# Three tiles of the first expert worked on ahead of the last routing, and the overflow loop inside a condition

## The chip, the core and the metric

One core of a Trainium2 chip runs the whole program in one launch. TensorE (PE) multiplies, its weight loads are listed as PEld; VectorE (DVE), ScalarE (ACT) and GpSimd (POOL) do the rest; SyncE (SP) and the queues of ACT and POOL issue DMAs. The metric is the device time of the launch in microseconds, the median of the runs. A measurement of this kernel tells two versions apart from about 0.2%, which is 2.1 us.

## The reference

Block-causal attention (4 batches, 8 heads, 576 positions, head size 64, blocks of 64) gives 2304 rows of 512. A mixture of experts sends each row to two of eight experts, and a gated MLP follows:

```python
attn = softmax(where(block_i >= block_j, scale * q @ k.T, -1e9)) @ v
x = attn as 2304 rows of 512
noisy = x @ w_gate + log1p(exp(x @ w_noise)) * noise
top2, top2_w = the two largest of 8, softmax over them
for e in range(8): out[mask] += top2_w * (maximum(x[mask] @ w1[e], 0) @ w2[e])   # 512 -> 1024 -> 512
h = out @ w_in                                                                   # 512 -> 2048
out = (h * clip(h + 3, 0, 6) / 6) @ w_out                                        # 2048 -> 512
```

## The kernel before

Everything is float32 on the outside. Each operand is split into a high and a low part (fp32r), and a product is three matmuls: high by high, low by high, high by low. A split is a copy on ACT (`split_hi`, `x_hi`, `h_hi`) and a subtraction on DVE (`split_lo`, `x_lo`, `h_lo`).

**Attention.** It runs over pairs of heads, batch by batch. Its order is not that of the code: each step is given to a `Plan` (a list scheduler in Python, run when the program is built) with its engine, an estimated cost, the steps that it needs and a priority (table `PR`); the plan writes the steps in the order that it finds, and that is the order of each engine's queue. When a batch is through, its gate logits are summed up (`lsum`, L858, in the tile `lgp`; matmuls `lgm`, L863 to L865) and its rows are routed (`route`). The attention's output rows are stored to the table `x_tok` in DRAM, from which rows are gathered by token number with indirect DMAs on POOL.

**The ahead stage.** The routing of the last batch is a long chain of small DVE steps. So that PE has work meanwhile, the first `AHEAD` tiles of expert 0 (128 rows each) are taken from the first three batches alone: `early_load` (L424) gathers them into `raw_q` and `raw_k`, buffers that the attention no longer needs, PE transposes them (`x_tr`, L401), and a second plan (`plan2`) interleaves expert 0's two matrix products over them with the last routing. A product has eight parts f of 128 hidden columns: `s1` (L433 to L435) is 12 matmuls per f, with the width of the tiles as their columns; `s2` (L1136 to L1138) three matmuls of 512 columns per f and tile. The remaining tiles of expert 0 (`load_x`, L1105, into `xn`) need the routing of all four batches; their gathers and transposes are at the end of `plan2`. Splits of the experts' weights into high and low (wa for the first matrix, wb for the second, by pairs of f) are steps of both plans; `PRE` says which of them the first plan makes.

**The experts.** 72 steps g (`NG`) follow, written out in code order: g = 0 to 7 is expert 0 over its remaining columns (624 are kept for it in all, `CAPS`), then experts 1 to 7, the last in two halves. The weights of the next expert are loaded in pairs from expert 0 on. A generator (`route_rows`, `rr` in the loop) makes, two pieces per step, the lists with which rows are turned later on, and the list of rows that are over an expert's capacity; `overflow_count` then loads their number into a register of every engine. **Overflow.** Just ahead of the last product of expert 7 (g = 72), `overflow()` runs a loop over those rows (L1254). For these inputs the number is zero, and the body never runs; the loop's branches and its waits do.

Last comes the MLP in five groups of rows.

Of the kernel before, what the change touches and what calls it, by code (L numbers as in the profile page):

```python
# [31 lines left out]
HB = 4  # L32
# [4 lines left out]
FIRST_TURNED = 2  # L37
TURN_X = (((), ()), ((), (0, 1)), ((), (2,)), ((0,), ()), ((1,), (3,)), ((2,), (4,)), ((3, 4), ()), ((), ()))
CONV = (8, 5)
STICK = 2.77  # L40
TURN = {(a, b): t for b, r in {"S": {"T": 0.045, "V": 0.083, "F": 0.086, None: 0.084}, "V": {"T": 0.134, "S": 0.072, "F": 0.086, None: 0.09},
                               "T": {"V": 0.038}}.items() for a, t in r.items()}
SELS = ({"DVE": 0.17}, {"POOL": 0.6}, {"DVE": 0.17, "POOL": 0.6}, {"POOL": 0.6, "DVE": 0.17})
PRE = ((0, 0), (1, 0))
WLS = ({"DVE": 1.2}, {"DVE": 1.14, "POOL": 2.4}, {"POOL": 2.4, "DVE": 1.14}, {"POOL": 2.4})
VHS = ({"POOL": 2.3}, {"DVE": 0.42}, {"POOL": 2.3, "DVE": 0.42}, {"DVE": 0.42, "POOL": 2.3}, {"ACT": 0.65, "DVE": 0.42})
PR = {'v': -317.22, 'qk': -13.33, 'keep': 1, 'S': -2.19, 'max': -82.24, 'exp': -40.31, 'pt': 0.29, 'hi': 360.75, 'lo': -37.22, 'hid': True, 'av': 7.35, 'o': 252.33, 'od': True, 'inv': 36.95, 'fin': 28.78, 'x': -1.53, 'route': -0.9, 'rp': 1, 'route2': 6.36, 'xt': 83.29, 'eg': 587.2, 'ex': 432.13, 'ew': 2149.25, 'first': 0, 'sel': 2, 'vh': 3, 'wl': 0, 'wa': -64.03, 'wb': 20.81, 'h': -79.68, 's2': -28.75, 'vs': (-0.62, -2.53, 0.92, 0.17, 0.59, -5.66), 'vpt': (28.74, 8.73, -37.77, -2.51, -5.17, 6.9, -0.23, 1.96), 'vp': (-2.81, -6.08), 'vf': (15.46, 3.5)}
CLAMP = 122879.9921875


# [7 lines left out]
class Plan:  # L58
# [97 lines left out]
def kernel(  # L156
# [15 lines left out]
    B, H, S, D = v.shape  # L172
# [5 lines left out]
    NF = F // 128  # L178
# [28 lines left out]
    k_in, k = k, {}  # L207
# [44 lines left out]
    NP2 = H // 2  # L252
# [46 lines left out]
    ohsum = [const.tile([128, E], BF16, name=f"ohsum{i}") for i in range(B)]  # L299
# [78 lines left out]
    w_s = {}  # L378
# [255 lines left out]
    with actx:  # L634
# [359 lines left out]
                                  lambda g: tb[g.bank],  # L994
                                  NU * NP2 * (b + 1) + PR["route2" if b == B - 2 else "route"])[0]
        for t in range(AHEAD):
            key = ("qk"[t], 0)
            k["eg", t] = add({"POOL": 1.04}, lambda e, t=t, key=key: early_load(t, raw[key]),
                             [k["r", B - 2], k["X", NPAIR - NP2 - 1]] + ([k["kl", NPAIR - 2]] if t else [k["ql", NPAIR - 2, h] for h in range(2)]), PR["eg"] + t, lat=2.4)
            g = Bank("t", PR["keep"])  # L1000
            tr = add({"PE": 0.44}, lambda e, t=t, g=g: x_tr("a", xn["a", t], t, AHEAD * 128, tb[g.bank].rearrange("p (k n) -> p k n", k=KD)), [k["eg", t]], PR["ex"] + t, take=g)
            hi_ = add({"ACT": 0.48}, lambda e, t=t, g=g: x_hi("a", t, tb[g.bank].rearrange("p (k n) -> p k n", k=KD)), [tr], PR["ex"] + t, drop=g)
            k["ex", t] = add({"DVE": 0.6}, lambda e, t=t, g=g: x_lo("a", t, tb[g.bank].rearrange("p (k n) -> p k n", k=KD)), [hi_], PR["ex"] + t, drop=g)
# [247 lines left out]

    def overflow():
        lst, nov, total = ovf["lst"], ovf["nov"], ovf["n"]
        with tc.For_i(0, total, 1) as j, tc.tile_pool(name="ov", bufs=1) as op_:  # L1254
            cur = op_.tile([128, 2], F32, name="cur")
            for r in range(2):
                nc.vector.tensor_copy(cur[:, r:r + 1], lst[:, r, bass.ds(j, 1)])
# [85 lines left out]
    k2 = {}  # L1343
# [22 lines left out]
    for f in range(NF + 1):  # L1366
        pr = 10 + 2 * f
        if f < NF and f % 2 == 0:
            k2["wa", f // 2] = wops(0, f // 2, [k2.get(("s1", f - 4 + i)) for i in range(2)], pr + PR["wa"])
        if f < NF and f % 2 == 0:  # L1370
            k2["wb", f // 2] = wops(1, f // 2, [k2.get(("s2", f - 4 + i)) for i in range(2)], pr + PR["wb"])
        if PR['first'] <= f < NF:
            g = Bank("h", 1)

            def first(e, f=f, g=g):
                g.tile = s1("a", f, f // 2, 0, n_)

            def second(e, f=f, g=g):
                hT["a", f] = h_tiles()
                h_hi(hT["a", f], g.tile, 0, n_)  # L1380

            k2["s1", f] = add({"PE": 1.31}, first, [k2.get(("wa", f // 2))], pr, take=g)
            hh = add({"ACT": 0.27}, second, [k2["s1", f], k2.get(("s2", f - HB))], pr + PR["h"], drop=g)
            k2["h", f] = add({"DVE": 0.34}, lambda e, f=f, g=g: h_lo(hT["a", f], g.tile, 0, n_), [hh], pr + PR["h"], drop=g)
        if f:
            k2["s2", f - 1] = add({"PE": 1.3}, lambda e, f=f - 1: s2(range(AHEAD), hT.pop(("a", f)), w_s[1, f // 2], f,
                                                                     f == 0, f == NF - 1),
                                  [k2.get(("h", f - 1)), k2.get(("wb", (f - 1) // 2)), k2.get(("s2", f - 2))], pr + PR["s2"])
    counts = work.tile([128, 16], F32, tag="counts", name="counts", bufs=1)[:, 0:E]
# [39 lines left out]
    wops(0, NPF, [k2["s1", NF - 4], k2["s1", NF - 3]], 50)
    wops(1, NPF, [k2["s2", NF - 4], k2["s2", NF - 3]], 51)  # L1430
# [11 lines left out]
    for g in range(NG + 1):  # L1442
        u = NPF + g // 2 + 1
        if g < NG:
            e, f, _, _ = STEPS[g]
            if g % 2 == 0:
                split(0, u)
            if f == 0 and e + 1 < E:
                for t in range(NT):
                    load_x(e + 1, t)  # L1450
            if wide and g == CONV[0] - 1:
                conv_load(0)
            if g % 2 == 1:
# [12 lines left out]
        if wide and g >= CONV[0]:
            for _ in range(CONV[1]):
                next(conv, None)
        if g == NG:
            overflow()  # L1470
        if g:
            e_s2(g - 1)
        if g == NG - NF:
            for t in range(len(GR[0])):
                gather(0, t)
        for _ in range(2):
            if next(rr, None) == 0:
                overflow_count()
        if g < NG and f >= 2 and f - 2 < NT and e + 1 < min(E, FIRST_TURNED):
            x_tile(e + 1, xn.pop((e + 1, f - 2)), f - 2, CAP)  # L1480
        if g < NG and FIRST_TURNED <= e + 1 < E:
            outs, ins = TURN_X[f]
            for t in outs:
                e_out(e + 1, t)
            for t in ins:
                e_in(e + 1, t)
        if NG - NF + 4 <= g < NG - NF + 4 + len(GR[0]):
            combine(0, g - (NG - NF + 4))
        if NG - NF + 5 <= g < NG - NF + 5 + len(GR[0]):
            combined(0, g - (NG - NF + 5))  # L1490
# [93 lines left out]
```

## Time and profile before

| | us |
|---|---|
| median of 3 runs (1068.59 to 1070.15) | 1069.24 |
| the profiled execution: own time | 1069.84 |
| its span, first to last instruction | 1068.0 |
| PE busy | 1051.7 |
| DVE busy | 778.2 |
| ACT busy | 593.3 |
| POOL busy | 316.5 |

The mean granted clock of TensorE in the span is 0.993. The profiled execution's own time is 1.84 us more than its span, and 0.60 us over the median. Times below are microseconds from the span's start. A row of the timeline gives start and duration; matmuls are pipelined, so a matmul of 256 columns is listed with 0.28 us and starts 0.12 us behind the one ahead of it. "[0.85 <-DMA xn...]" means that the engine sat idle 0.85 us before this instruction, and what released it.

### The profile page before, as it was taken

What the parts mean: (1) busy time and instruction counts of PE and PEld (TensorE: products, weight loads), DVE (VectorE), ACT (ScalarE), POOL (GpSimd) and SP (SyncE); (2) the same over time, 40 slices, a digit from 0 to 9 for tenths busy, and PEclk for the clock granted to TensorE, in tenths of its full rate; (3) what the DMA queues carried; (4) which work ended last, traced back from release to release, by engine and by line L of the source; (5) the groups of instructions that cost most, each with busy time, mean ns of one, the idle gap of its engine ahead of it and who ended that gap; (6) DMA issues with size and microseconds to landing.
All of it is one profiled execution on the core that took longest, in us unless ns stands there. A gap on an engine that the chain in (4) does not pass through costs nothing. (4 is left out here: it accounts for less than half of the span.)

```text
span 1068.0 us, 16961 instructions
## 1 busy us (share of the span) xinstructions
PE 1051.7 (98%) x6069; PEld 923.8 (86%) x6069; DVE 778.2 (73%) x1471; ACT 593.3 (56%) x1121; POOL 316.5 (30%) x378
## 2 busy tenths in 40 slices
PE   8999999999999999999999999999999999999998
PEld 6999999987988999999888898988888888888886
DVE  8878787887598898988787855875745755665442
ACT  6777777764456555655555444654535444454442
POOL 7558787723101120202020001743401421310000
PEclk8999999999999999999999999999999999999999
DMA  7534432114999999987787525212202211201001
GB/s 185 148 96 129 130 90 53 24 47 150 328 275 331 301 301 280 278 225 255 195 247 202 165 82 176 79 60 60 56 5 69 50 40 48 62 10 40 1 1 40
DMA packets 163573, 141.80 MB, mean 133 GB/s; under 512 B 92373, under 2 KB 131381, under 8 KB 163485
## 3 DMA queue, kind: packets, MB, share of 16 engines
q1 hardware_dynamic: 147501, 102.79, 34.7%
q0 software_dynamic: 8640, 28.32, 8.5%
q10 hardware_dynamic: 7344, 9.57, 2.7%
q8 instruction: 49, 0.80, 0.3%
q14 instruction: 39, 0.32, 0.1%
HBM read 92.94 MB, written 36.70 MB: 121 GB/s over the span
## 5 line engine op out<-in xcount | busy, mean ns | idle before, releaser
L433 PE MATMUL h<-xh,wah 128*128 128x512 f32 (+8 forms) x832 | 272.7, 328 | 0.7 <-ACT xh L404 0.7
L434 PE MATMUL h<-xl,wah 128*128 128x512 f32 (+8 forms) x832 | 271.5, 326 | 0.4 <-issue 0.3
L435 PE MATMUL h<-xh,wal 128*128 128x512 f32 (+8 forms) x832 | 271.5, 326 | 0.0
L1136 PE MATMUL y<-wbh,hh 128*128 128x512 f32 (+1 forms) x576 | 226.3, 393 | 2.1 <-issue 2.1
L1137 PE MATMUL y<-wbl,hh 128*128 128x512 f32 (+1 forms) x576 | 226.0, 392 | 0.0
L1138 PE MATMUL y<-wbh,hl 128*128 128x512 f32 (+1 forms) x576 | 225.5, 392 | 0.0
L433 PEld LDWEIGHTS h<-xh,wah 128*128 128x128 f32 x832 | 156.6, 188 | 16.2 <-ACT xh L404 1.0
L434 PEld LDWEIGHTS h<-xl,wah 128*128 128x128 f32 x832 | 156.7, 188 | 15.5 <-issue 0.5
L435 PEld LDWEIGHTS h<-xh,wal 128*128 128x128 f32 x832 | 156.6, 188 | 11.5
L1138 PEld LDWEIGHTS y<-wbh,hl 128*128 128x128 f32 (+1 forms) x576 | 107.6, 187 | 25.4 <-DVE hl L460 0.8
L1136 PEld LDWEIGHTS y<-wbh,hh 128*128 128x128 f32 (+1 forms) x576 | 107.5, 187 | 23.3 <-issue 2.5
L456 ACT ACTIVATE hh<-h 128x288 fp32r<-128x288 f32 (+7 forms) x128 | 53.0, 416 | 132.1 <-PE h L435 130.9
L1137 PEld LDWEIGHTS y<-wbl,hh 128*128 128x128 f32 (+1 forms) x576 | 107.6, 187 | 20.6
L1498 DVE SCALAR_TENSOR_TENSOR r<-r,h 128x512 f32<-128x512 f32 (+1 forms) x80 | 50.5, 631 | 97.9 <-ACT r L1497 97.7
L1497 ACT ACTIVATE r<-h,three 128x512 f32<-128x512 f32 (+1 forms) x80 | 51.6, 645 | 120.2 <-PE h L435 120.1
L388 DVE TENSOR_TENSOR wal<-wa,wah 128x1024 fp32r<-128x1024 f32 x80 | 106.3, 1328 | 12.1 <-ACT wah L384 10.9
L388 DVE TENSOR_TENSOR wbl<-wb,wbh 128x1024 fp32r<-128x1024 f32 x76 | 102.5, 1349 | 14.6 <-ACT wbh L384 12.8
L384 ACT CAST wbh<-wb 128x1024 fp32r<-128x1024 f32 x80 | 83.8, 1048 | 23.4 <-PE y L1138 13.3
L1501 DVE TENSOR_TENSOR hl<-r,hh 128x512 fp32r<-128x512 f32 (+1 forms) x80 | 57.3, 717 | 51.5 <-ACT hh L1500 51.0
L1500 ACT CAST hh<-r 128x512 fp32r<-128x512 f32 (+1 forms) x80 | 46.2, 577 | 84.7 <-DVE r L1498 83.2
L772 ACT ACTIVATE P<-sb,nm 128x192 f32<-128x192 f32 (+4 forms) x144 | 74.6, 528 | 28.8 <-DVE nm L766 28.8
L384 ACT CAST wah<-wa 128x1024 fp32r<-128x1024 f32 x80 | 83.7, 1046 | 3.0 <-DMA wb<-in_moe_w_dram 2.4
(269 smaller groups left out, 1783.3 us busy)
## 6 DMA issues: line engine op xcount, KB each, us to landing
wa<-in_moe_w_dram SPq DMA_DIRECT2D x23, 512.0 KB
wb<-in_moe_w_dram SPq DMA_DIRECT2D x23, 512.0 KB
y_tab<-yo SPq DMA_DIRECT2D x32, 256.0 KB
w<-in_moe_w_in_dram SPq DMA_DIRECT2D x16, 512.0 KB
y_tab<-zero SPq DMA_DIRECT2D x8, 1024.0 KB
w<-in_moe_w_out_dram SPq DMA_DIRECT2D x16, 512.0 KB
x_tok<-x SPq DMA_DIRECT2D x32, 144.0 KB
wa<-in_moe_w_dram ACTq DMA_DIRECT2D x9, 512.0 KB
```

The lines of the kernel that those rows point to most:

```text
L384: nc.scalar.copy(w_s[which, u][0], raws[PS[u]][which])
L388: (nc.gpsimd if e == "POOL" else nc.vector).tensor_tensor(lo, raws[PS[u]][which], hi.bitcast(F32), op=OP.subtract)
L433: nc.tensor.matmul(ps, lhsT=wh, rhs=xh, start=first, stop=False)
L434: nc.tensor.matmul(ps, lhsT=wh, rhs=xl, start=False, stop=False)
L435: nc.tensor.matmul(ps, lhsT=wl, rhs=xh, start=False, stop=last)
L456: nc.scalar.activation(h[0][:, c0:c1], ps[:, :c1 - c0], AF.Relu)
L772: nc.scalar.activation(o, views.pop((p, i)), AF.Exp, bias=nms.pop((p, i)), scale=1.0, accum_out=rs[p % 3][:, i:i + 1])
L1136: nc.tensor.matmul(yps[t][:n], lhsT=hh[:, sl], rhs=wh[:, f % 2], start=first, stop=False)
L1137: nc.tensor.matmul(yps[t][:n], lhsT=hh[:, sl], rhs=wl[:, f % 2], start=False, stop=False)
L1138: nc.tensor.matmul(yps[t][:n], lhsT=hl[:, sl], rhs=wh[:, f % 2], start=False, stop=last)
L1497: nc.scalar.activation(r[:, :n], ps[:, :n], AF.Relu, bias=three, scale=1.0)
L1501: nc.vector.tensor_tensor(hl[:, :n], r[:, :n], hh[:, :n].bitcast(F32), op=OP.subtract)
```

## The change

- `AHEAD` is 3: a third tile is gathered, into the buffer `raw_v`, once the high and low parts of the pair before the last are made from it, and is part of the ahead stage. `s1` there has 384 columns and `s2` nine matmuls per f; expert 0 after the routing has 240 columns in place of 368, and two late gathers in place of three.
- `PRE` loses (1, 0): the low and high part of the first pair of the second matrix is made in `plan2` and not in the attention.
- Priorities in `PR`: the last batch's routing -75 (before -1000), the ranks 0 (before -900), the last `s1` -30, the late transposes -9 (before 83.29). Costs that the plan assumes for `s1`, `s2` and the splits grow with the width; the assumed latency of the late gathers is 3.6 (before 2.4).
- `RR` = 8: `route_rows` starts at step g = 8.
- The overflow loop is inside `tc.If(total > 0)`.

```diff
-AHEAD = 2
+AHEAD = 3
...
+RR = 8
...
-PRE = ((0, 0), (1, 0))
+PRE = ((0, 0),)
...
     def early_load(t, a):
+        if len(a.shape) > 2:
+            a = a.rearrange("p c h d -> p (c h d)")
...
         for t in range(AHEAD):
-            key = ("qk"[t], 0)
+            key = ("qkv"[t], 0)
+            free = ([k["ql", NPAIR - 2, h] for h in range(2)], [k["kl", NPAIR - 2]], [k["hi", NPAIR - 2], k["lo", NPAIR - 2]])[t]
             k["eg", t] = add({"POOL": 1.04}, lambda e, t=t, key=key: early_load(t, raw[key]),
-                             [k["r", B - 2], k["X", NPAIR - NP2 - 1]] + ([k["kl", NPAIR - 2]] if t else [k["ql", NPAIR - 2, h] for h in range(2)]), PR["eg"] + t, lat=2.4)
+                             [k["r", B - 2], k["X", NPAIR - NP2 - 1]] + free, PR["eg"] + t, lat=2.4)
...
-        with tc.For_i(0, total, 1) as j, tc.tile_pool(name="ov", bufs=1) as op_:
+        with tc.If(total > 0), tc.For_i(0, total, 1) as j, tc.tile_pool(name="ov", bufs=1) as op_:
...
-            k2["s1", f] = add({"PE": 1.31}, first, [k2.get(("wa", f // 2))], pr, take=g)
+            k2["s1", f] = add({"PE": 12 * (n_ / 2400.0 + 0.0145)}, first, [k2.get(("wa", f // 2))], pr if f < NF - 1 else PR["s1"], take=g)
...
-            k2["s2", f - 1] = add({"PE": 1.3}, lambda e, f=f - 1: s2(range(AHEAD), hT.pop(("a", f)), w_s[1, f // 2], f,
+            k2["s2", f - 1] = add({"PE": 0.69 * AHEAD}, lambda e, f=f - 1: s2(range(AHEAD), hT.pop(("a", f)), w_s[1, f // 2], f,
...
-    _, dp = route(B - 1, [], add, lambda: Bank("x", 1), psum, -1000, plan.done[k["lg", B - 1]])
+    _, dp = route(B - 1, [], add, lambda: Bank("x", 1), psum, PR["last"], plan.done[k["lg", B - 1]])
...
-        k2["g", t] = add({"POOL": 1.04}, lambda e, t=t: load_x(0, t), [dp["id"]], -10 + t, lat=2.4)
+        k2["g", t] = add({"POOL": 1.04}, lambda e, t=t: load_x(0, t), [dp["id"]], -10 + t, lat=3.6)
...
-        for _ in range(2):
+        for _ in range(2 if g >= RR else 0):
             if next(rr, None) == 0:
                 overflow_count()
```

The order of GpSimd's queue at the end of the attention: the last sums `lgp` of the gate logits, the early gathers (`raw_q`, `raw_k`, `raw_v`) and the first late gathers. Before:

```order
L585 TENSOR_SCALAR sel_3153<-laneb,pmf 128x128
L424 DMA raw_q_74<-x_tok,ids_152 128x512
L424 DMA raw_k_76<-x_tok,ids_152 128x512
L858 TENSOR_TENSOR lgp_205<-lgp_205,x 64x144 x2
L1017 MEMSET capv 128x1 x8
L1105 DMA xn<-x_tok,ids 128x512 x3
```

And of the change:

```order
L588 TENSOR_SCALAR sel_3153<-laneb,pmf 128x128
L861 TENSOR_TENSOR lgp_205<-lgp_205,x 64x144 x2
L427 DMA raw_q_74<-x_tok,ids_152 128x512
L427 DMA raw_k_76<-x_tok,ids_152 128x512
L427 DMA raw_v_72<-x_tok,ids_152 128x512
L1021 MEMSET capv 128x1 x8
L1109 DMA xn<-x_tok,ids 128x512 x2
```

The two sums stand ahead of the gathers now, a third gather behind them, and two late gathers are left.

TensorE's queue at the same place, where the attention's last transposes (L840, L843 now) end and the ahead stage begins. Before:

```order
L840 MATMUL tb_172<-iw,oT_3257 128x96 x5
L401 MATMUL tb_168<-ident,raw_q_74 128x128 x4
L401 MATMUL tb_171<-ident,raw_k_76 128x128 x4
L863 MATMUL tb_169<-lgp_205,half 128x16
L864 MATMUL tb_169<-lgp_205,half 128x64
L865 MATMUL tb_169<-lgp_205,half 128x64
L433 MATMUL h<-xh_3292,wah_3139 128x256
```

And of the change:

```order
L843 MATMUL tb_172<-iw,oT_3254 128x96 x5
L402 MATMUL tb_168<-ident,raw_q_74 128x128 x4
L402 MATMUL tb_171<-ident,raw_k_76 128x128 x4
L866 MATMUL tb_169<-lgp_205,half 128x16
L867 MATMUL tb_169<-lgp_205,half 128x64
L868 MATMUL tb_169<-lgp_205,half 128x64
L402 MATMUL tb_170<-ident,raw_v_72 128x128 x4
L436 MATMUL h<-xh_3289,wah_3139 128x384
```

The transpose of the third tile stands between the logits and the first product, whose matmuls all read the three tiles together.

TensorE's queue behind the overflow loop, where the last product of expert 7 begins. Before:

```order
L1254 REGISTER_ALU
L1254 COMPARE_AND_BRANCH
L1254 UNCONDITIONAL_BRANCH [waits DMASW5_49,DMASW4_49,DMASW6_49,DMASW3_49,DMASW7_49,DMASW2_49,DMAHW0_49,DMASW1_49,DMAHW1_49,DMASW0_49,DMAHW2_49,SP_sequencer_49,DMAHW3_49,DVE_sequencer_49,DMAHW4_49,PE_sequencer_49,DMAHW5_49,Activation_s
L1136 MATMUL y_7935<-wbh,hh 128x512
```

And of the change:

```order
L1258 UNCONDITIONAL_BRANCH [waits PE_49]
L1140 MATMUL y_7933<-wbh,hh 128x512 [waits Activation_49]
L1141 MATMUL y_7933<-wbl,hh 128x512
L1142 MATMUL y_7933<-wbh,hl 128x512 [waits DVE_49]
```

With the loop skipped, the branch that waits for every engine and DMA queue lies on the path of before; on that of the change lies one that waits for PE's own semaphore, and the first matmuls have waits of their own.

## Rows read from the trace of the kernel before

**Rows 1.** The page: busy time and its share of the span by engine.

```profile
PE 1051.7 (98%) x6069; PEld 923.8 (86%) x6069; DVE 778.2 (73%) x1471; ACT 593.3 (56%) x1121; POOL 316.5 (30%) x378
```

**Rows 2.** Busy time by stretch: PE, PEld, DVE, ACT, POOL, granted clock, DMA share, GB/s.

```profile
220.00:230.00 10.00, 9.26 (x77) 8.72 (x75) 6.81 (x18) 4.72 (x10) 4.34 (x12) 1.00 0.34 86
250.00:260.00 10.00, 8.04 (x47) 6.45 (x47) 7.09 (x12) 3.96 (x7) 8.08 (x7) 1.00 0.65 187
658.00:660.00 2.00, 0.02 (x1) 0.00 (x0) 0.44 (x2) 0.00 (x0) 0.00 (x0) 1.00 0.06 12
```

**Rows 3.** Timeline of POOL, end of the attention.

```profile
220.54 1.22 POOL L424 DMA_INDIRECT raw_q<-x_tok,ids  x1 [5.61 <-DVE ri L827]
222.07 0.94 POOL L424 DMA_INDIRECT raw_k<-x_tok,ids  x1 [0.31 <-issue]
223.04 1.39 POOL L858 TENSOR_TENSOR lgp<-lgp,x 64x144 f32<-64x144 f32 x1
225.99 0.49 POOL L858 TENSOR_TENSOR lgp<-lgp,x 64x144 f32<-64x144 f32 x1 [1.56 <-DMA raw_k<-x_tok,ids]
```

**Rows 4.** Timeline of DVE, beside these.

```profile
222.33 0.55 DVE L847 TENSOR_TENSOR x<-tb,ri 128x384 f32<-128x384 f32 x1
222.92 1.17 DVE L388 TENSOR_TENSOR wbl<-wb,wbh 128x1024 fp32r<-128x1024 f32 x1
```

**Rows 5.** Timeline of PE, start of the ahead stage.

```profile
227.56 0.60 PE L401 MATMUL tb<-ident,raw_q 128*128 128x128 f32 x4
228.00 0.60 PE L401 MATMUL tb<-ident,raw_k 128*128 128x128 f32 x4
229.15 0.40 PE L863 MATMUL tb<-lgp,half 128*128 128x16 f32 x2 [0.55 <-DVE lgp L858]
230.47 0.39 PE L434 MATMUL h<-xl,wah 128*128 128x256 f32 x1
```

**Rows 6.** Timeline of POOL: the first late gather.

```profile
248.63 1.15 POOL L1105 DMA_INDIRECT xn<-x_tok,ids  x1 [21.80 <-PE y L1138]
```

**Rows 7.** Timeline of PE, end of the ahead stage.

```profile
248.44 0.28 PE L433 MATMUL h<-xh,wah 128*128 128x256 f32 x1
...
251.12 0.28 PE L435 MATMUL h<-xh,wal 128*128 128x256 f32 x1
252.25 0.66 PE L401 MATMUL xps<-ident,xn 128*128 128x128 f32 x4 [0.85 <-DMA xn<-x_tok,ids]
...
254.38 0.66 PE L401 MATMUL xps<-ident,xn 128*128 128x128 f32 x4
...
256.26 0.60 PE L401 MATMUL xps<-ident,xn 128*128 128x128 f32 x4
257.59 0.43 PE L433 MATMUL h<-xh,wah 128*128 128x368 f32 x1 [0.73 <-ACT xh L404]
258.31 0.43 PE L434 MATMUL h<-xl,wah 128*128 128x368 f32 x1 [0.29 <-issue]
```

**Rows 8.** Timeline of PE at the overflow loop.

```profile
657.63 0.39 PE L1138 MATMUL y<-wbh,hl 128*112 128x512 f32 x1
660.10 0.68 PE L1136 MATMUL y<-wbh,hh 128*128 128x512 f32 x1 [2.08 <-issue]
```

**Rows 9.** PE's sequencer at line L1254: ns min/median/max, first and last start.

```profile
L1254 PEldq EVENT_SEMAPHORE  x13: 51/51/51, 658.1 to 659.7; - x13
L1254 PEldq COMPARE_BRANCH  x3: 101/187/319, 655.4 to 659.9; - x3
```

**Rows 10.** Busy time by stretch (columns as in rows 2): below full clock.

```profile
660.00:662.00 2.00, 1.90 (x5) 1.48 (x6) 0.00 (x0) 0.33 (x1) 0.00 (x0) 0.56 0.01 4
662.00:664.00 2.00, 2.00 (x11) 1.79 (x10) 1.05 (x2) 1.20 (x2) 0.00 (x0) 0.58 0.34 131
8.00:12.00 4.00, 2.44 (x13) 1.42 (x12) 3.39 (x9) 3.29 (x12) 1.86 (x2) 0.97 0.84 222
12.00:22.00 10.00, 8.40 (x33) 7.43 (x33) 9.10 (x17) 5.47 (x16) 8.18 (x9) 0.50 0.52 123
```

More of the change, by code (lines that the diff above doesn't have):

```diff
@@ L43 @@
 SELS = ({"DVE": 0.17}, {"POOL": 0.6}, {"DVE": 0.17, "POOL": 0.6}, {"POOL": 0.6, "DVE": 0.17})
-PRE = ((0, 0), (1, 0))
+PRE = ((0, 0),)
 WLS = ({"DVE": 1.2}, {"DVE": 1.14, "POOL": 2.4}, {"POOL": 2.4, "DVE": 1.14}, {"POOL": 2.4})
 VHS = ({"POOL": 2.3}, {"DVE": 0.42}, {"POOL": 2.3, "DVE": 0.42}, {"DVE": 0.42, "POOL": 2.3}, {"ACT": 0.65, "DVE": 0.42})
-PR = {'v': -317.22, 'qk': -13.33, 'keep': 1, 'S': -2.19, 'max': -82.24, 'exp': -40.31, 'pt': 0.29, 'hi': 360.75, 'lo': -37.22, 'hid': True, 'av': 7.35, 'o': 252.33, 'od': True, 'inv': 36.95, 'fin': 28.78, 'x': -1.53, 'route': -0.9, 'rp': 1, 'route2': 6.36, 'xt': 83.29, 'eg': 587.2, 'ex': 432.13, 'ew': 2149.25, 'first': 0, 'sel': 2, 'vh': 3, 'wl': 0, 'wa': -64.03, 'wb': 20.81, 'h': -79.68, 's2': -28.75, 'vs': (-0.62, -2.53, 0.92, 0.17, 0.59, -5.66), 'vpt': (28.74, 8.73, -37.77, -2.51, -5.17, 6.9, -0.23, 1.96), 'vp': (-2.81, -6.08), 'vf': (15.46, 3.5)}
+PR = {'last': -75, 'ranks': 0, 's1': -30, 'v': -317.22, 'qk': -13.33, 'keep': 1, 'S': -2.19, 'max': -82.24, 'exp': -40.31, 'pt': 0.29, 'hi': 360.75, 'lo': -37.22, 'hid': True, 'av': 7.35, 'o': 252.33, 'od': True, 'inv': 36.95, 'fin': 28.78, 'x': -1.53, 'route': -0.9, 'rp': 1, 'route2': 6.36, 'xt': -9, 'eg': 587.2, 'ex': 432.13, 'ew': 2149.25, 'first': 0, 'sel': 2, 'vh': 3, 'wl': 0, 'wa': -64.03, 'wb': 20.81, 'h': -79.68, 's2': -28.75, 'vs': (-0.62, -2.53, 0.92, 0.17, 0.59, -5.66), 'vpt': (28.74, 8.73, -37.77, -2.51, -5.17, 6.9, -0.23, 1.96), 'vp': (-2.81, -6.08), 'vf': (15.46, 3.5)}
 CLAMP = 122879.9921875
@@ L1380, in second @@
                 h_hi(hT["a", f], g.tile, 0, n_)
-            k2["s1", f] = add({"PE": 1.31}, first, [k2.get(("wa", f // 2))], pr, take=g)
-            hh = add({"ACT": 0.27}, second, [k2["s1", f], k2.get(("s2", f - HB))], pr + PR["h"], drop=g)
-            k2["h", f] = add({"DVE": 0.34}, lambda e, f=f, g=g: h_lo(hT["a", f], g.tile, 0, n_), [hh], pr + PR["h"], drop=g)
+            k2["s1", f] = add({"PE": 12 * (n_ / 2400.0 + 0.0145)}, first, [k2.get(("wa", f // 2))], pr if f < NF - 1 else PR["s1"], take=g)
+            hh = add({"ACT": 0.06 + n_ / 1200.0}, second, [k2["s1", f], k2.get(("s2", f - HB))], pr + PR["h"], drop=g)
+            k2["h", f] = add({"DVE": 0.08 + n_ / 960.0}, lambda e, f=f, g=g: h_lo(hT["a", f], g.tile, 0, n_), [hh], pr + PR["h"], drop=g)
         if f:
-            k2["s2", f - 1] = add({"PE": 1.3}, lambda e, f=f - 1: s2(range(AHEAD), hT.pop(("a", f)), w_s[1, f // 2], f,
+            k2["s2", f - 1] = add({"PE": 0.69 * AHEAD}, lambda e, f=f - 1: s2(range(AHEAD), hT.pop(("a", f)), w_s[1, f // 2], f,
                                                                      f == 0, f == NF - 1),
@@ L1419 @@
         add({"ACT": 0.6} if t % 2 else {"DVE": 0.6}, lambda e, t=t: y_out(0, t), [k2["s2", NF - 1]], 100)
-    _, dp = route(B - 1, [], add, lambda: Bank("x", 1), psum, -1000, plan.done[k["lg", B - 1]])
+    _, dp = route(B - 1, [], add, lambda: Bank("x", 1), psum, PR["last"], plan.done[k["lg", B - 1]])
     gn = Bank("x", 1)
     c_ = add({"PE": 0.1}, lambda e: nc.tensor.matmul(psum(gn)[:, 0:E], lhsT=ones, rhs=ohsum[B - 1], start=True, stop=True),
-             [dp["ohsum"]], -900, take=gn)
-    c_ = add({"DVE": 1.6}, lambda e: ranks(psum(gn)), [c_], -900, drop=gn, port=True)
+             [dp["ohsum"]], PR["ranks"], take=gn)
+    c_ = add({"DVE": 1.6}, lambda e: ranks(psum(gn)), [c_], PR["ranks"], drop=gn, port=True)
     add({"DVE": 1.1}, lambda e: slot_rows(), [c_, dp["id"]], PR["xt"] + 20, port=True)
     for t in range(AHEAD, NT):
-        k2["g", t] = add({"POOL": 1.04}, lambda e, t=t: load_x(0, t), [dp["id"]], -10 + t, lat=2.4)
+        k2["g", t] = add({"POOL": 1.04}, lambda e, t=t: load_x(0, t), [dp["id"]], -10 + t, lat=3.6)
         xops(t, k2["g", t], PR["xt"] + t)
```

## The prediction

> **What bounds the kernel now.** I read the page first: PE is busy for 1051.7 of 1068.0 us [rows 1], so 16.3 us of the span are all that PE's idle time can give, and the rest could only go with fewer matmuls or a higher clock. The change keeps every matmul of the kernel. So the question is which of the idle stretches it closes, which it opens, and what the clock does around them. The windows by stretch came second. Three stretches bear on the change: the end of the attention and the start of the ahead stage (0.74 us idle in 220 to 230), the end of the ahead stage (1.96 us in 250 to 260), and the overflow loop (1.98 us in 658 to 660) [rows 2]. Then came the timelines of these places, to see what PE waits for. At the end of the ahead stage it waits for the first late gather, later for the copies of the transposed tile [rows 7]. At the overflow loop the idle 2.08 us are put down to "issue" [rows 8], which says that no engine's work ended the wait; PE's sequencer shows what it did: 13 semaphore events, the last at 659.7, and branches, the last at 659.9 [rows 9]. [...]
>
> **The overflow loop.** With the loop skipped, the change leaves out the block in which every engine waits for all the others and all queues, and PE keeps one wait for its own semaphore. The first event is at 658.1 and takes 0.05; PE's branches at this line take 0.10 to 0.32 [rows 9]. Add one branch of that kind and the next product starts between 658.25 and 658.55, not at 660.10 [rows 8]: 1.55 to 1.85 us less, and I take 1.6, since the longest branch may be the one that jumps. What stays is a gap of some 0.3 to 0.5 us. What PE has to wait for then is the high part of the last hidden columns, done on ACT before, and the low part on DVE, wanted by the third matmul only. Now the clock. PE's idle time of 2.08 us is followed by 3.90 us of busy PE at 0.56 and 0.58: 1.90 x 0.44 + 2.00 x 0.42 = 1.68 us lost [rows 10]. Does a gap of 0.5 us bring the clock down too? The stretch 250 to 260 has gaps of 0.85 and 0.73 us [rows 7] and a clock of 1.00 throughout [rows 2], so I say no, and count all of 1.68 as gained. Together 3.28 us; the bounds are 0 (the jump costs what the waits cost, and the clock falls as before) and 3.5.
>
> [...]
>
> **The start of the ahead stage.** GpSimd's order changes: the two sums stand ahead of the gathers. The first sum reads an x that DVE ends at 222.88 [rows 4], so it cannot start before about 223.0, where it starts now too [rows 3]. The gathers were issued at 220.54 and 222.07. Now the sums come first: 0.49 us is what a sum takes alone, 1.39 what the one beside DVE's `wbl` took [rows 3, 4]; that `wbl` is what `PRE` drops, so I take 0.5 to 0.7 each, and the first gather is issued at 223.04 + 1.0 to 1.4 + 0.3 = 224.3 to 224.7. The next two follow at 0.94 + 0.31 = 1.25 each [rows 3], so the third at 226.8 to 227.2. Landing: the late gather issued at 248.63 releases PE at 252.25, 3.62 later [rows 6, 7]; `raw_k`, issued at 222.07, ends a wait at 225.99, 3.92 later [rows 3]. So `raw_v` is there at 230.4 to 231.1. From a transpose to the second matmul of the product behind it (which needs DVE's low part) it took 256.26 to 258.31 = 2.05 [rows 7]. PE is then at that second matmul at 232.5 to 233.15, not at 230.47 [rows 5]: 2.0 to 2.7 later. One transposed tile, 0.44 (227.56 to 228.00) [rows 5], has moved here from the late stage and is no loss: 1.6 to 2.25, and I take **+1.9**. Bounds: if both sums take 1.39, the gathers are some 1.7 later, +3.6; below, 0, if a gather lands early enough for other work to cover it, for which I see no row.
>
> **The ahead stage itself.** The columns are only parted in another way (256 and 368 before, 384 and 240 now, 624 both times), and the numbers of matmuls are the same. 24 matmuls of 256 columns start from 248.44 to 251.12 [rows 7]: 2.68 / 23 = 0.1165 us each, with no room for a fixed cost that another parting would change by much; zero. The split of the first `wb` pair moves behind the first three `s1`, which is 36 matmuls, 36 x 0.175 = 6.3 us by columns; against DVE's 1.17 for a `wbl` [rows 4], hidden. If it were not, its 1.17 would be paid once.
>
> **The end of the ahead stage.** Idle by the starts [rows 7]: from 251.12 to 252.25, 1.13 less one matmul of 0.12, 1.01. From 252.25 to 254.38 (a transposed tile and six matmuls of `s2`) 2.13, where the same from 254.38 to 256.26 took 1.88: 0.25. From 256.26 to 257.59, 1.33 less 0.41 for the four transposes: 0.92. From 257.59 to 258.31, 0.72 less 0.17: 0.55. Sum 2.73. The change puts more work ahead of this: 96 `s1` matmuls get 128 columns more (0.058 each by the pace above, 5.6 us) and 24 matmuls of 512 columns are new (0.233 each, 5.6 us), 11.2 in all. The routing starts some 0.6 us later (the logits' matmuls wait for the second early tile, not for DVE), and with its priority cut more of DVE's splits stand between its steps; even 6 us more on that way leave the gathers landed before PE asks. In the order of the change the last two `s2` stand behind the two late transposes, 18 matmuls x 0.233 = 4.2 us, more than the 2.05 that copies and low parts take. So the 2.73 go: **-2.7**, with 0 as the bound if the routing is later by all of 11.
>
> **At no cost.** `RR` moves small DVE pieces and the load of the number by eight steps of 72; PE does not wait for DVE in those steps, and the number is wanted at the 72nd. The weights of expert 1 are loaded behind the ahead stage, some 10 us later, with expert 0's remaining columns and its second product as cover.
>
> **Sum**, against the profiled execution's own 1069.84: +1.9 - 2.7 - 3.28 = -4.1, so 1065.75. That execution is 0.60 over the median, so against the median of 1069.24: **1065.2**.
>
> **The rivals.**
>
> *B, the clock falls at the start of the ahead stage.* From the last attention transposes to about 232.7 PE would have the transposes of three tiles, the logits and little more: some 2 us of work in 5. The trace has both outcomes for thin work. In 8 to 12 PE is busy 2.44 of 4.00, and behind it the clock is 0.50 for ten microseconds; in 250 to 260 it is busy 8.04 of 10 and the clock stays [rows 10, 2]. If it falls for as long as behind the overflow loop, 1.68 are lost: 1066.9.
>
> *C, the early gathers are hidden,* since the attention's own end is later than I read, or the sums take less: +1.9 becomes 0, and the time is 1063.3. Against it: the second sum now waits at 225.99 and all it needs besides is there.
>
> [...]
>
> *E, slower.* B, but the clock stays low as it does from 12 to 22, ten microseconds, with PE busy all the time: 10 x 0.5 = 5.0 lost, and -4.1 becomes +0.9, 1070.1. It decides on the sign from 8.2 us of low clock, and on a difference that can be measured (0.2%, 2.1 us) from 12.5. For it, 8 to 12 is as thin as the new stretch; against it, PE is still idle for 1.60 of the ten microseconds from 12 to 22, and here 36 matmuls follow one another.
>
> **How the numbers follow.** The forecast 0.40, B 0.34, C 0.08, D 0.09, E 0.07, and 0.02 for what I don't see. The time is the forecast's, 1065.2. The range takes in C at its low end, and B with its bounds and half of D at its high end: 1063.3 to 1068.2. A difference of 0.2%, 2.1 us, is about what a measurement of this kernel can tell from none: faster is below 1067.1, slower above 1071.4. The forecast and C are faster; B lies at the edge, so two thirds of it; D and the rest of B are "same", and E parts between "same" and "slower". With what both unknowns together may do, 0.71, 0.23 and 0.06.
>
> **What would show it.** At the overflow place: a gap of 0.3 to 0.5 us ahead of the first matmul of the last product, no low clock behind it. At the end of the ahead stage: no wait for `xn` or for the high parts. At its start: the early gathers behind the sums at 224.3 to 224.7, the first product's second matmul at about 232.7, and the clock just behind it, which tells the forecast from B and E. Wrong would be: `raw_v` landing before 229 or after 232; a wait of over 1 us for `xn`; a jump of over 1 us; a wait for weights of expert 1 from 290 on.

## The result, and the profile after

| | us |
|---|---|
| before, median of 4 runs (1068.59 to 1070.15) | 1068.94 |
| the change, median of 4 runs (1075.23 to 1077.54) | 1076.14 |
| ratio, 95% interval | 1.0069, 1.0057 to 1.0082 |
| the change's profiled execution: own time, span | 1077.54, 1075.7 |

The change is 7.2 us slower, where 4.0 us faster was forecast (1069.24 to 1065.2). PE has the same matmuls as in [rows 1]; the windows of the profile after show where it stood still or ran at half clock (columns as in [rows 2]):

```profile
PE 1055.4 (98%) x6069; PEld 926.1 (86%) x6069; DVE 777.4 (72%) x1471; ACT 592.8 (55%) x1121; POOL 314.2 (29%) x378
```

```profile
220.00:230.00 10.00, 8.89 (x72) 8.27 (x73) 5.40 (x16) 3.51 (x9) 4.39 (x13) 1.00 0.41 109
230.00:240.00 10.00, 8.80 (x43) 8.13 (x43) 6.26 (x18) 6.04 (x10) 0.00 (x0) 0.83 0.14 32
250.00:260.00 10.00, 10.00 (x60) 9.04 (x59) 7.68 (x24) 2.47 (x4) 2.32 (x3) 1.00 0.08 23
...
300.00:350.00 50.00, 45.20 (x260) 39.93 (x259) 42.91 (x94) 29.36 (x41) 2.78 (x4) 0.93 1.00 290
```

The kernel before, in the last of these stretches:

```profile
300.00:350.00 50.00, 50.00 (x306) 44.60 (x305) 45.36 (x98) 30.66 (x46) 8.67 (x10) 1.00 1.04 307
```

The stretch 250 to 260 has lost its idle time, as forecast. The start of the ahead stage has more, with a clock of 0.83 in 230 to 240, which is case B. The last stretch is the one that the prediction had not priced: 4.80 us of idle PE and a clock of 0.93 where the kernel before was never idle. The timelines, first of POOL and PE at the start of the ahead stage (answering to [rows 3, 5]):

```profile
222.81 1.05 POOL L861 TENSOR_TENSOR lgp<-lgp,x 64x144 f32<-64x144 f32 x2 [8.03 <-DVE x L850]
224.17 1.22 POOL L427 DMA_INDIRECT raw_q<-x_tok,ids  x1 [0.30 <-POOL lgp L861]
225.69 0.94 POOL L427 DMA_INDIRECT raw_k<-x_tok,ids  x1 [0.31 <-issue]
226.94 0.95 POOL L427 DMA_INDIRECT raw_v<-x_tok,ids  x1 [0.30 <-issue]
```

```profile
230.71 0.66 PE L402 MATMUL tb<-ident,raw_v 128*128 128x128 f32 x4 [0.28 <-DMA raw_v<-x_tok,ids]
232.04 0.48 PE L436 MATMUL h<-xh,wah 128*128 128x384 f32 x1 [0.68 <-ACT xh L405]
232.76 0.69 PE L437 MATMUL h<-xl,wah 128*128 128x384 f32 x1 [0.25 <-DVE xl L410]
...
668.00 0.39 PE L1142 MATMUL y<-wbh,hl 128*112 128x512 f32 x1
668.53 0.47 PE L1140 MATMUL y<-wbh,hh 128*128 128x512 f32 x1
```

The last two rows answer to [rows 8]: the gap at the overflow place is 0.53 less a matmul's 0.23, 0.30 us in place of 2.24. Then the new wait, in PE's, ACT's and DVE's timelines:

```profile
300.00 0.29 PE L438 MATMUL h<-xh,wal 128*128 128x272 f32 x1
305.08 0.60 PE L436 MATMUL h<-xh,wah 128*128 128x272 f32 x1 [4.80 <-DVE hl L463]
```

```profile
294.20 0.37 ACT L459 ACTIVATE hh<-h 128x240 fp32r<-128x240 f32 x1
301.05 0.38 ACTq L350 DMA_DIRECT2D wa<-in_moe_w_dram  x1
301.95 0.38 ACTq L352 DMA_DIRECT2D wb<-in_moe_w_dram  x1
302.37 1.04 ACT L385 CAST wah<-wa 128x1024 fp32r<-128x1024 f32 x1 [7.80 <-issue]
```

```profile
303.45 1.23 DVE L389 TENSOR_TENSOR wal<-wa,wah 128x1024 fp32r<-128x1024 f32 x1 [7.57 <-ACT wah L385]
```

PE's row names DVE's `hl` as its releaser; but DVE itself had waited 7.57 us for ACT's `wah`, the first split of expert 1's next pair, and ACT, free since 294.57, for "issue": nothing that computes. The bytes that this split reads were not late: they landed at 281.26. What stands between on ACT's queue is the issue of a weight load for expert 2 at 301.05. In the program it waits for a DMA semaphore that an earlier load uses:

```
L350 DMA wa<-in_moe_w_dram 128x4x256 [waits DMAHW2_49,DVE_49]
L352 DMA wb<-in_moe_w_dram 128x2x512 [waits DMAHW5_49,DVE_49]
L385 CAST wah<-wa 128x1024
```

The DMA completions recorded in the trace tell which: the load `wa` issued on the same semaphore at 289.71 has its sixteenth and last at 300.91, 11.2 us later. In this trace the 19 DMA issues of ACT and the 341 of SyncE carry the same eight semaphores, DMAHW0 to DMAHW7, in the program one after another. Between the loads at 289.71 and 291.01 and the blocked issue, SyncE issued six pieces of a zero fill (spare rows of the table `y_tab`, 293.29 to 298.81), each with a semaphore of its own. That makes eight, and the blocked issue carries the one of 289.71 again.

In the kernel before, the loads issued from 284 to 292 landed after 4.7 to 6.1 us. The same kind of block is there already, shorter (2.39 us), and PE, busy for all 38.00 us from 262 to 300, does not feel it:

```profile
291.47 0.38 ACTq L351 DMA_DIRECT2D wb<-in_moe_w_dram  x1
291.89 1.05 ACT L384 CAST wah<-wa 128x1024 fp32r<-128x1024 f32 x1 [2.39 <-DMA wb<-in_moe_w_dram]
```

What surrounds the slow loads, two windows show. They are the ahead stage and expert 0's remaining columns, before:

```profile
236.00:256.00 20.00, 19.06 (x134) 16.36 (x133) 17.79 (x73) 7.55 (x13) 5.93 (x5) 1.00 0.16 45
262.00:300.00 38.00, 38.00 (x220) 34.22 (x219) 24.10 (x51) 16.24 (x25) 4.94 (x6) 1.00 0.97 314
```

and after:

```profile
236.00:256.00 20.00, 20.00 (x117) 17.98 (x116) 17.53 (x68) 8.20 (x13) 0.00 (x0) 1.00 0.00 0
262.00:300.00 38.00, 36.28 (x236) 31.33 (x234) 20.86 (x28) 16.07 (x26) 9.16 (x10) 1.00 0.92 311
```

From the first load of expert 1 on, the DMA engines are almost full (share 0.97 before, 0.92 after); in the ahead stage of the change they do nothing (share 0.00 in 236 to 256). The longer ahead stage moves that first load from 261.61 to 271.85.

**The account**, span 1068.0 to 1075.7: start of the ahead stage +1.85 (232.76 for 230.47, less 0.44 for the tile moved), half clock behind it +1.6 (1.80 us of busy PE at 0.88 in 230 to 233, 3.00 at 0.55 to 236), end of the ahead stage -2.7, three waits between 275 and 291 +1.7, the wait at 300 +4.8, half clock behind it +2.9 (rows below), the overflow place -3.6. Sum +6.5 of 7.7; the other 1.2 are not placed.

```profile
304.00:306.00 2.00, 0.92 (x4) 0.92 (x5) 1.97 (x6) 1.49 (x3) 0.00 (x0) 0.50 0.88 298
306.00:308.00 2.00, 2.00 (x11) 2.00 (x11) 1.90 (x4) 0.35 (x2) 0.00 (x0) 0.50 1.07 306
308.00:310.00 2.00, 2.00 (x6) 1.61 (x6) 1.93 (x6) 1.79 (x3) 0.00 (x0) 0.50 0.99 351
310.00:312.00 2.00, 2.00 (x8) 1.55 (x8) 2.00 (x6) 1.44 (x2) 0.00 (x0) 0.80 0.97 365
```

### The profile page after: what moved, and what is told of

Same layout as the page of the kernel before. It is cut to its first block, busy times and chain, and to the rows that moved or that the text cites. A ratio compares the mean times of both kernels' runs of the same rounds, so it can differ in the third digit from the quotient of the medians.

```text
span 1075.7 us, 16931 instructions
## 1 busy us (share of the span) xinstructions
PE 1055.4 (98%) x6069; PEld 926.1 (86%) x6069; DVE 777.4 (72%) x1471; ACT 592.8 (55%) x1121; POOL 314.2 (29%) x378
## 5 line engine op out<-in xcount | busy, mean ns | idle before, releaser
L436 PE MATMUL h<-xh,wah 128*128 128x512 f32 (+7 forms) x832 | 273.9, 329 | 5.5 <-DVE hl L463 4.8
L437 PE MATMUL h<-xl,wah 128*128 128x512 f32 (+7 forms) x832 | 272.5, 328 | 0.2 <-DVE xl L410 0.2
L438 PE MATMUL h<-xh,wal 128*128 128x512 f32 (+7 forms) x832 | 272.6, 328 | 0.0
L1141 PE MATMUL y<-wbl,hh 128*128 128x512 f32 x576 | 226.2, 393 | 0.2
L1140 PE MATMUL y<-wbh,hh 128*128 128x512 f32 x576 | 226.1, 393 | 0.1
L1142 PE MATMUL y<-wbh,hl 128*128 128x512 f32 x576 | 225.5, 391 | 0.5 <-DVE hl L463 0.5
L459 ACT ACTIVATE hh<-h 128x288 fp32r<-128x288 f32 (+5 forms) x128 | 53.1, 416 | 141.3 <-PE h L438 136.8
L1142 PEld LDWEIGHTS y<-wbh,hl 128*128 128x128 f32 x576 | 107.6, 187 | 25.9 <-DVE hl L463 1.0
L1141 PEld LDWEIGHTS y<-wbl,hh 128*128 128x128 f32 x576 | 107.8, 187 | 21.6 <-POOL wbl L389 0.8
L1140 PEld LDWEIGHTS y<-wbh,hh 128*128 128x128 f32 x576 | 107.8, 187 | 21.2 <-issue 0.6
```

Of the source, the lines that this page charges most:

```text
L436: nc.tensor.matmul(ps, lhsT=wh, rhs=xh, start=first, stop=False)
L437: nc.tensor.matmul(ps, lhsT=wh, rhs=xl, start=False, stop=False)
L438: nc.tensor.matmul(ps, lhsT=wl, rhs=xh, start=False, stop=last)
L459: nc.scalar.activation(h[0][:, c0:c1], ps[:, :c1 - c0], AF.Relu)
L1140: nc.tensor.matmul(yps[t][:n], lhsT=hh[:, sl], rhs=wh[:, f % 2], start=first, stop=False)
L1141: nc.tensor.matmul(yps[t][:n], lhsT=hh[:, sl], rhs=wl[:, f % 2], start=False, stop=False)
```

## The experiments

Theory 1: ACT's queue is blocked by load issues that wait for earlier loads. Theory 2: the bytes that PE needs are late themselves. After the first four runs, theory 3: the DMA engines are full from expert 1's first load on, a later start leaves too little room, and the blocked queue is only where that shows first.

**1. Loads on SyncE from g = 4.**

```diff
-                load_raw(r + 1, nc.scalar if g < 10 else None)
+                load_raw(r + 1, nc.scalar if g < 4 else None)
```

> The change with one edit: the loads of expert weights at steps g = 4 to 9 are issued by SyncE's queue, not by ScalarE's. Theory 1 (ScalarE's in-order queue: an issue that waits for an earlier load to land stands ahead of the split that PE needs): the 4.80 us of idle PE at 300.3 and the half clock behind it (6.8 us at 0.5, 3.4 lost) go, the loads land no earlier, and the time is 1076.1 - 8.2 = about 1068. Theory 2 (the bytes themselves are late, DMA bandwidth): the split would have to wait anyway, and the time stays at 1075 to 1077.

1073.16 us, 1.0036 (1.0023 to 1.0049) of before. The 4.80 us are gone and a wait of 3.5 us is there at 283:

```profile
283.37 1.11 PE L402 MATMUL xps<-ident,xn 128*128 128x128 f32 x4 [3.50 <-DVE xl L410]
```

```profile
281.58 0.38 ACTq L352 DMA_DIRECT2D wb<-in_moe_w_dram  x1
282.00 0.58 ACT L405 CAST xh<-xps 128x512 fp32r<-128x512 f32 x1 [6.57 <-DMA wa<-in_moe_w_dram]
```

The same picture: ACT's copy of a transposed tile stands behind an issue that waits for a load, and ACT sits idle 6.57 us before it. In the program the issue at 281.58 waits for DMAHW7, which SyncE's second `wa` for expert 2 uses just before it. So the blocked queue is real, and the time fell by 3, not by 8.

**2, 3. The condition.** The change without `tc.If`, and the kernel before with it alone.

```diff
-        with tc.For_i(0, total, 1) as j, tc.tile_pool(name="ov", bufs=1) as op_:
+        with tc.If(total > 0), tc.For_i(0, total, 1) as j, tc.tile_pool(name="ov", bufs=1) as op_:
```

> The change without the condition: the bare overflow loop as before. If the condition is worth what the two traces show (the gap ahead of the last product of 0.30 in place of 2.24 us, and no half clock behind it, 1.68), this is 3.6 us slower than the change, about 1079.7. If the difference of the gaps comes from the other edits (the number of overflow rows loaded 8 steps later), no change: 1076.

> The kernel before with the condition alone. By the same reading -3.6 us: about 1065.3, with a gap of about 0.3 us and full clock behind it. Rival: in this kernel the number is loaded early and the wait is shorter, so less than 2 us.

The change without it: 1077.24 us, 1.0070 (1.0057 to 1.0083) of before, where the change had 1.0069: no difference between them that these runs can tell. The kernel before with it: 1066.86, 0.9978 (0.9968 to 0.9989), 2.3 us less (1.2 to 3.4). Both expectations of 3.6 were too high. The windows 655 to 675 tell why: the first without the condition (experiment 2), then with it alone (3), then the control of experiment 4, without it.

```profile
655.00:675.00 20.00, 17.86 (x111) 15.74 (x110) 11.72 (x17) 9.18 (x16) 1.31 (x2) 0.91 0.45 153
```

```profile
655.00:675.00 20.00, 19.85 (x134) 17.80 (x133) 13.42 (x21) 10.93 (x19) 9.58 (x7) 1.00 0.31 92
```

```profile
655.00:675.00 20.00, 17.85 (x119) 16.00 (x118) 12.82 (x20) 10.81 (x18) 8.62 (x7) 1.00 0.30 86
```

The gap of about 2.1 us is there in the first and the third, yet the clock falls in the first (0.91) only. Of four profiled executions with this gap (before, experiments 2, 4 and 12) it fell in two: 0.57 in 660 to 664 in before, 0.91 over the 20 us of experiment 2, and 1.00 behind the gap in experiments 4 and 12. So 1.94 us of gap are certain, and the 1.68 us of clock are paid in some executions.

**4. Control: the loads of experiment 1 in the kernel before.**

> The kernel before with the loads of steps g = 4 to 9 issued by SyncE. Control for the first run: PE never waits for the splits in this kernel, so by theory 1 the time does not change (within 0.5 us of 1069). If moving the loads helps by itself, for another reason, it shows here.

1069.90, 1.0013 (1.0004 to 1.0022): a little slower, if anything. Moving the issues does not help here, where PE is busy for all of 262 to 300 without it.

**5. All loads on SyncE** (`load_raw(r + 1)` at every step).

> The change with all loads of expert weights on SyncE, so ScalarE's queue holds no DMA issue in expert 0. The bytes and their order are the same. Theory 1 (an issue that waits for the landing of the load that used its semaphore before it blocks ScalarE): no wait of PE over 1 us between 270 and 340, and about 1076.1 - 4.8 - 3.4 = 1068 at best; in the first run, where ScalarE kept the first eight issues, the stall moved to one of them (3.5 us at 283). Theory 2 (the weights land too late, DMA bandwidth): PE waits for a split that waits for a load, 2 us or more, and 1072 or more.

1071.69, 1.0027 (1.0016 to 1.0037). No wait is left up to 300, and two come later (rows: engine, line, releaser, us in total, times, longest):

```profile
PE h L436 <- DVE hl L463: 2.0, 1, 2.0
PE y L1136 <- DVE yo L1153: 0.9, 1, 0.9
```

Between the two expectations: with ACT's queue free, 2.9 us of wait remain. DVE's queue has taken the place of ACT's: it stands 3.57 us to 298.19 and 3.48 us to 309.27 for `w`, weights of the last MLP, with `yo` and the split and `hl` behind it:

```profile
DVE ca L1042 <- DMA w<-in_moe_w_in_dram: 7.1, 2, 3.6
```

Theory 1, a block of ACT's queue, is true of the 4.80 us and not the whole.

**6. Expert 2's loads four steps later.**

```diff
-        load_at.setdefault(max(2 * (last_use[r - 8] - NPF) if r >= 8 else 0, r - NPF), []).append(r)
+        load_at.setdefault(max(2 * (last_use[r - 8] - NPF), r - NPF + 4) if r >= 8 else r - NPF, []).append(r)
```

> The change with expert 2's loads four steps later (g = 8 to 11 in place of 4 to 7), issued by SyncE; expert 1's four pairs stay on ScalarE. Fewer loads are in flight, so both the block on ScalarE and the demand for bandwidth go. Theory 1 and theory 2 alike: no wait in 270 to 340 and about 1068; if even this leaves a wait, the cause is neither, and 1072 or more.

1074.01, 1.0052 (1.0038 to 1.0066): a miss. The DMA engines stand partly free in 262 to 300 and are full later, and PE waits in both stretches:

```profile
262.00:300.00 38.00, 34.68 (x225) 30.04 (x224) 22.96 (x33) 18.16 (x30) 9.26 (x10) 1.00 0.81 260
300.00:340.00 40.00, 40.00 (x252) 35.94 (x251) 33.72 (x76) 23.24 (x32) 2.03 (x3) 1.00 1.03 296
340.00:400.00 60.00, 57.89 (x343) 52.00 (x343) 51.97 (x114) 35.08 (x50) 9.33 (x11) 1.00 1.10 324
```

The waits in the first stretch are no matter of a full share (0.81). Expert 1's loads are still issued by ACT, and its copies stand behind them: behind an issue that takes 3.57 us, and behind one that waits for a load of SyncE's (issued at 272.88, landed at 284.40):

```profile
280.18 0.59 ACT L405 CAST xh<-xps 128x512 fp32r<-128x512 f32 x1 [4.10 <-issue]
284.84 0.59 ACT L405 CAST xh<-xps 128x512 fp32r<-128x512 f32 x1 [2.86 <-DMA wb<-in_moe_w_dram]
```

In the later stretch PE's wait of 1.06 us at 346.33 goes back, over ACT and DVE, to DMA transposes that came late (ACT waits 1.64 us for `xn` to 341.71, where the DMA share is 1.10). Only this part of the run agrees with theory 3.

**7. The early gathers first** (experiment 6, and one sum of the gate logits on DVE).

```diff
-            k["ls", p] = add({"DVE": 0.6} if last else {"POOL": 1.1},
+            k["ls", p] = add({"DVE": 0.6} if p >= NPAIR - 2 else {"POOL": 1.1},
```

> The run before it in this list, and the last sum of the gate logits but one moved from GpSimd to DVE, so that the three early gathers stand at the head of GpSimd's queue, at about 220.5 to 223. If the 2.3 us at the start of the ahead stage come from the gathers' place behind the sums, PE's gaps at 229 to 233 shrink to under 1 us and the half clock behind them goes: 1.9 + 0 to 1.7 us less than that run, about 1065. Rival: the third buffer comes free too late, or the sum on DVE delays the last rows: no difference.

1070.42, 1.0026 (1.0017 to 1.0035): 0.0026 of before, or 2.8 us, under experiment 6; the 1065 rested on a base of 1068 that experiment 6 did not reach. The waits for the gathers are gone and the clock stays; experiment 6's row stands first, this one's second:

```profile
224.00:240.00 16.00, 13.89 (x83) 12.86 (x82) 8.74 (x24) 7.72 (x14) 3.41 (x11) 0.89 0.34 88
```

```profile
224.00:240.00 16.00, 15.06 (x94) 13.81 (x92) 12.68 (x48) 8.03 (x14) 0.00 (x0) 1.00 0.21 50
```

**8, 9. Expert 1's loads ahead,** on GpSimd's queue behind the late gathers, the others on SyncE at their old steps; experiment 9 has the edit of 7 too.

```diff
+    load_raw(2 * NPF, nc.gpsimd)
     for g in range(NG + 1):
...
-                load_raw(r + 1, nc.scalar if g < 10 else None)
+                load_raw(r + 1)
```

> The change with expert 1's four pairs of loads issued by GpSimd behind the last late gather of expert 0, when the ahead stage's tiles come free (about 263 in place of 271.85 and on), and the loads of expert 2 and on by SyncE at their old steps. Theory 3 (the DMA engines are full from the first of these loads to about 430, so a later start makes PE wait in the end, whichever queue issues): the DMA stretch starts 8 to 9 us earlier, PE's waits between 270 and 400 (6.5 us in the change, 3 to 5 us in the runs that only moved or spread the loads) fall under 1 us, and the time is 1076.1 - 6.5 - 3.4 + 0.5 = about 1066.7. Theory 1 alone (only the block of ScalarE's queue): the same as with all loads on SyncE, 1071.7.

> The same, and the sum of the gate logits on DVE, so that the early gathers come first. By theory 3 and the run with early gathers: 1066.7 - 1.9 to 3.6 = about 1064, under the kernel before with the condition alone (1066.9). If it is not under that, the third tile is worth nothing even without its two side effects.

1067.84, 0.9998 (0.9988 to 1.0007), and 1064.43, 0.9965 (0.9951 to 0.9979). The edit of experiment 8 differs from that of 5 in the time and the queue of these four pairs alone: their eight issues run from 258.8 to 264.3, with semaphores that SyncE and ACT do not use (DMASW0 to DMASW7). Which of the two counts, the earlier time or the other queue, was not tried. The loads that SyncE issues from 270 to 286 still take 8.4 to 14.5 us to land, so slow loads alone do not make PE wait. Its only wait in 262 to 400 is 1.2 us for a gather (first row); experiment 9 has none (its windows below):

```profile
PE xps L402 <- DMA xn<-x_tok,sids: 1.2, 1, 1.2
```

```profile
262.00:300.00 38.00, 38.00 (x256) 34.24 (x256) 28.10 (x45) 20.92 (x33) 11.73 (x13) 1.00 0.99 353
300.00:340.00 40.00, 40.00 (x245) 35.67 (x245) 36.85 (x84) 23.29 (x34) 4.81 (x6) 1.00 1.08 315
```

**10. The zero fill 30 steps later,** everything else as in the change, loads on ACT too.

```diff
-        if g > NF and g % 3 == 0 and g // 3 - NF // 3 <= OVF // 4:
-            zero_rows(g // 3 - NF // 3 - 1)
-        if g == NF:
+        z = g - 30
+        if z > NF and z % 3 == 0 and z // 3 - NF // 3 <= OVF // 4:
+            zero_rows(z // 3 - NF // 3 - 1)
+        if z == NF:
```

> The change with the zero fill of the table's spare rows (8 writes of about 1 MB from 293 on, then one each 3 steps) put 30 steps later; loads on ScalarE as in the change. Theory 3: the fill takes DMA time in the full stretch, without it the load that the blocked issue waits for lands earlier, and the 4.80 us at 300 shrink to under 2.5; time 1070 to 1073. Theory 1 in the narrow form (number of loads on ScalarE alone): the 4.80 us stay, 1076.

1068.56, 0.9997 (0.9987 to 1.0006): 7.6 us under the change, and 1.4 us under the low end of what theory 3 gave. With ACT's issues where they were, the wait at 300 is gone altogether:

```profile
300.00:340.00 40.00, 40.00 (x246) 35.55 (x245) 37.16 (x83) 24.59 (x34) 2.78 (x4) 1.00 0.85 245
```

Fewer bytes are not what the trace shows as the reason. The six pieces ahead of 300 are 704 KB of the 11.80 MB that the change moves in 262 to 300; the writes of 1 MB follow from 309 on. Without them the DMA share of the stretch is no lower; the change stands first, experiment 10 second:

```profile
272.00:300.00 28.00, 26.28 (x176) 22.49 (x174) 14.26 (x19) 11.65 (x19) 5.72 (x6) 1.00 0.99 346
```

```profile
272.00:300.00 28.00, 27.41 (x183) 23.76 (x183) 20.58 (x33) 15.56 (x28) 5.49 (x5) 1.00 1.06 383
```

The loads issued from 280 to 291 still take 9.5 to 11.6 us to land (11.2 to 12.3 in the change, 282 to 291). What differs more is the semaphore. The eighth `wa`, blocked to 301.05 in the change by the `wa` just ahead of it, here gets the semaphore of a load issued at 276.91, which landed at 287.24, and goes out at 289.97; the split behind it waits 0.84 us:

```profile
289.97 0.38 ACTq L350 DMA_DIRECT2D wa<-in_moe_w_dram  x1
292.30 1.05 ACT L385 CAST wah<-wa 128x1024 fp32r<-128x1024 f32 x1 [0.84 <-issue]
```

No run keeps the bytes and changes the semaphores alone, so the two are not parted by an experiment.

This run also kept its clock at the start of the ahead stage (1.00 in 224 to 240), with the same gaps as experiment 6: that fall, too, is not paid in every execution. It was in six of the seven profiled ones with these gaps: mean clock 0.89 in 224 to 240 in the change and experiments 5, 6 and 8, and 0.93 and 0.86 in 215 to 240 in experiments 1 and 2.

**11, 12. All three edits; and the later fill in the kernel before.**

> Early gathers first, expert 1's loads ahead, and the zero fill 30 steps later. By theory 3 the loads ahead already took every wait between 262 and 400 away, so the later fill gives nothing more: the same as that run, 1064.4 within 1 us. If the fill costs by itself (its writes on the way of others'), 1 to 3 us less.

> Control: the kernel before with the zero fill 30 steps later. PE has no wait between 262 and 430 in it, so by theory 3 no change (within 1 us of before). A gain like that of the same edit in the change (7.6 us) would say that the fill costs for another reason.

1063.96, 0.9951 (0.9937 to 0.9964), and 1068.22, 0.9996 (0.9987 to 1.0005). The control shows no gain where PE does not wait. Experiment 11 is the fastest version: 5.1 us under its own runs of before (median 1069.03). Its interval and that of experiment 9 overlap.

## Why the prediction was wrong

**The step that failed** stands under "At no cost": "The weights of expert 1 are loaded behind the ahead stage, some 10 us later, with expert 0's remaining columns and its second product as cover." The 10 us were right (271.85 for 261.61). The cover was named and never measured. Two things were wrong with it. The change takes 128 columns out of the very stage that was to be the cover, so its eight steps need less time while they still bring the same loads; and those loads already kept the DMA engines almost full (0.97 of 262 to 300 in the kernel before, a row that the prediction did not use). The wait at 300, those at 275 to 291 and the half clock behind are 9.4 us of the account.

That the wait at 300 arises on ACT's queue, at an issue ahead of a split whose bytes had long landed, is shown by the change's own rows and by experiments 1 and 5. By the runs it takes two things: loads that need 11 us (11.2 and 11.6 for the two of 289.71 and 291.01), and an issue on a computing queue that must wait for a load issued shortly before (at 289.71, with ACT free for the issue from 294.57). In the kernel before, the loads needed 4.7 to 6.1 us and the block of 2.39 us cost PE nothing. Experiment 8 has loads about as slow (8.4 to 14.5 us) and no issue on ACT; experiment 10 has loads nearly as slow (9.5 to 11.6 us), but its issue gets the semaphore of an older load. Neither has the wait at 300. That full DMA engines alone make PE wait (theory 3 as it was put) is not shown: in the kernel before, the share is 1.04 in 300 to 350 and PE never idles. Why the loads are so much slower in the change is argued from the crowding of that stretch, and no run shows it by itself.

The prediction did put "a wait for weights of expert 1 from 290 on" among the things that would make it wrong, which has the place right and the mechanism not, and gave it no price: it should have been a rival, on the slower side.

**The start of the ahead stage** went as worked out: gathers at 224.17, 225.69 and 226.94 (224.3 to 224.7 and 226.8 to 227.2 were forecast), the second matmul at 232.76 (232.5 to 233.15). Of forecast and B, the chip gave B in most executions; its price of 1.68 measured 1.6. Experiment 7 shows the cause of the waits, the sums ahead of the gathers; the clock stayed at 1.00 in it, as in experiment 9 with the same edit.

**The end of the ahead stage** went as forecast: no wait for `xn` or the high parts in 250 to 270.

**The overflow place**: the gap of 0.3 to 0.5 us measured 0.30, with full clock behind it. The mis-sized term is the 1.68 of the clock, counted in full although one execution had shown it: the condition alone is worth 2.3 us (1.2 to 3.4) and not 3.28. In the change the difference cannot be told from none. D, in the range and the chances, is a smaller gain at this place; no run shows the size it was given. The profile of the change shows in its place: PE's longest branch there took 357 ns, and behind the gap that stays the clock is 1.00 (660 to 680).

```profile
L1258 PEldq COMPARE_BRANCH  x1: 357/357/357, 665.7 to 665.7; - x1
```

**Open**: 1.2 us of the account; what makes the clock fall behind the same gap in one execution and not in the next; and whether the mends of experiments 7, 8 and 10 would serve two tiles as well as three, which was not tried. Experiments 9 and 11 say that with them three tiles beat both kernels, not that the third tile is the reason. Against the kernel before with the condition alone (0.9968 to 0.9989) the interval of experiment 9 overlaps, and that of experiment 11 lies just below.

## What to carry to other kernels

When a change lengthens one stage and shortens the next, look at what the next stage has to bring in, not only at what PE waits for now. Here loads at a DMA share of 0.92 to 0.97, started 10 us later, came back as waits. ACT's queue, which issues loads and also computes, was held up by the loads; its wait of 7.80 us put down to "issue", behind a DMA issue, was a wait for an earlier transfer. Which transfer that was depended on the semaphore that the issue got, and so on what SyncE issued in between: the load of 289.71 with six pieces of the fill ahead, one of 276.91 in experiment 10 without them. And a clock loss seen in one profiled execution, here in two of four, is a chance, not a term.

## What the runs showed of the hardware

Behind the same gap of about 2.1 us, followed by the same matmuls, the clock fell in two profiled executions of four (before: 0.56 and 0.58 in 660 to 664; experiment 2: 0.91 in 655 to 675), and was 1.00 in the others (experiments 4 and 12). A weight load of 512 KB took 4.7 to 6.1 us from issue to landing at the end of expert 0 before (issued from 284 to 292, a stretch with a DMA share of 0.90 and 281 GB/s), and 11.2 to 11.6 us in the change (issued from 285 to 291; in 284 to 292 the share is 1.06, with 384 GB/s). The issue itself took longer there too: 0.38 to 0.40 us on ACT's queue before, and 1.08 to 1.91 us in the change.
